# Retention, gated FFN and experts on one core: VectorE's and GpSimd's share of the side work, q's decay tables, and the pacing of the FFN

## The chip, the cores and the metric

One core of a Trainium2 chip runs the whole program. The metric is the device time of one execution in microseconds (us). Engines: PE is TensorE (PEld its weight loads), DVE is VectorE, ACT is ScalarE, POOL is GpSimd, SP is SyncE, whose queue issues almost every DMA. A matmul writes a PSUM bank of 128 x 512 floats; in this kernel VectorE and ScalarE read PSUM, and GpSimd works in SBUF alone.

## The reference

Three steps, each on the output of the one before:

```python
for t in range(S):                       # B=2, H=8, S=768, D=64
    state = gamma[None, :, None, None] * state + k_t v_t^T
    y[:, :, t] = scale * q_t @ state
x = y as (1536, 512)
xn = x / sqrt(mean(x * x) + 1e-6) * rms_g
x = (silu(xn @ w_gate) * (xn @ w_val)) @ w_out        # d_ff = 1536
p = probs / (probs.sum(-1) + 1e-9)                    # 4 experts, F = 1024
out = sum over e of p[:, e] * (relu(x @ w1[e]) @ w2[e])
```

## The kernel before, in words

The recurrence is computed in chunks of 128 tokens: 2 batches of 6 chunks, twelve in all (`NS`), i = 0 to 11. In each step i the program issues the scores of chunk i+1 (q times k, L631), masks them by VectorE (`am`, L639), and then mixes chunk i: masked scores times v (L660) plus q times the state S (L652), and the state's update (L688, copied to S by ScalarE, L696). Decay by position is kept in tables: `gk` scales k (L609), and `gq`, one 128 x 512 table for each of the last five chunks of a batch, scales q in place (`prep_q`, L620, by VectorE or GpSimd). The five `gq` tables come by five DMAs on SP's queue (L793, L826).

The norm of a chunk (`normal`, `normal2`) is a chain between ScalarE and VectorE: square and sum L674, root L676 and L678, VectorE's reciprocal L703, ScalarE's L706 to L708, and VectorE's product `xn` L714. `to_x` then transposes xn on PE (L736) into one of six PSUM banks, which are used in turn. The matmuls of the FFN are made from operands split in two: a high part (cast to fp32r) and a low part (value minus high part), so each product of two matrices is three matmuls. The tokens of a batch form two blocks of 384. A product over two blocks and two halves of the weights is done with seven smaller products instead of eight (the Winograd form, L449), which needs sums of pieces: `first` holds block 0 as copied out of PSUM (L745), `tsum` holds differences (L758, L760, L766, L770), and xX, xB22 and xT are the split operands (high L722 and L756, low L725 and L762; L725 is `split`).

Each weight tile arrives as 64-bit numbers in `wst` and is turned into high and low parts by a sequence: bits L301 (ScalarE); L304, L309, L315 and L322 `top` (VectorE); sums L338 and low parts `widelo`/`plainlo` L371 (VectorE or GpSimd); casts L366 (ScalarE). ScalarE's L458 copies a product's bank to `kept`; VectorE's L539, L509 and L542 add and multiply the products, L513 is the Silu, and L547 the low part of h. The output products are L966 to L968.

The order of such side work is written by a planner in the program, `Pace` (L32 to L137). It keeps a clock for each engine, moved on by `did` and `work` with costs from `COST`, and a clock `now` for PE, moved on by `matmuls`. Tasks wait in lists with the engines that may do them ("PV" is GpSimd or VectorE). `fill(span)` issues tasks that are ready and end within the span; `need` issues a task that must be done now, on the engine whose clock and cost are least. `ready` counts back a latency where a task follows one of its own engine. A task that uses the port that VectorE and GpSimd share (`port`) also starts no earlier than the other engine's last such task. Nothing is chosen at run time: the planner sets the order in which instructions stand on each engine.

The last two norms and the first products of the FFN overlap: from chunk 10 on, the first FFN unit's gate products fill PE between the mixes. The FFN has six units (`N1`) for each of two batches, twelve steps; the experts follow.

Of the kernel before, what the change touches and what calls it, by code (L numbers as in the profile page):

```python
# [31 lines left out]
class Pace:  # L32
# [6 lines left out]
    COST = {"A": (0.09, 0.00085), "V": (0.07, 0.00105), "P": (0.14, 0.00213), "D": (0.0, 0.0018)}  # L39
# [4 lines left out]
    def __init__(self, engines):  # L44
        self.engines = engines

        self.order = "DVAP"
        self.now = 0.0
        self.clock = dict.fromkeys("AVPD", 0.0)

        self.port = {"V": 0.0, "P": 0.0}
        self.waiting = [[], [], []]

    def cost(self, engine, size):
        fixed, each = self.COST[engine]
# [31 lines left out]
    def need(self, *tasks):  # L87

        for task in tasks:
            if task.end is None:  # L90
                self.need(*task.deps)
                engine = min(task.engines, key=lambda e: self.clock[e] + self.cost(e, task.size))
# [3 lines left out]
    def ready(self, task, engine):  # L96

        ends = [d.end - (self.LATENCY[engine] if d.engine == engine else 0.0) for d in task.deps]
# [4 lines left out]
    def can(self, task, engine):  # L103
        return (
# [49 lines left out]
def tile_retention_gated_experts(  # L154
# [16 lines left out]
    c_q: bass.AP,  # L171
    out: bass.AP,
# [11 lines left out]
    H = c_k.shape[2]  # L184
    S = NCH * CHUNK
# [379 lines left out]
    with ExitStack() as actx:  # L565
# [11 lines left out]

        rows = [wstage.tile([P, H, CHUNK], F32, tag="wst", name=f"rows{x}")[0:1] for x in range(2)]
        g_sb = ac.tile([P, DM], F32, name="g_sb")
# [8 lines left out]
        first_block = {}  # L588
# [25 lines left out]
        def prep_q(i):  # L614

            c = chunks[i][1]
            if c:
# [3 lines left out]
                    [pace.done(pace.now)],  # L621
                )

        def scores(i):
# [8 lines left out]
            st[i]["scores"], st[i]["am"] = ps, am  # L633
            prep_q(i)
# [95 lines left out]
        def to_x(i):  # L730
# [8 lines left out]
            if blk == 0:  # L739
# [4 lines left out]
                hi, lo = (x[:, :, cols] for x in xs[b]["X"])  # L744
                nc.scalar.copy(out=b1, in_=ps)  # L745
                done = pace.done(pace.did("A", DM))
                split(b, first_block[b, "readers"], [done], hi, lo, b1, DM)
# [37 lines left out]
        nc.scalar.dma_start(out=square, in_=c_square)  # L785
        nc.vector.memset(S_sb[0], 0.0)
# [6 lines left out]
        nc.sync.dma_start(out=gq[:, 0], in_=c_q[:, 0])  # L793
# [24 lines left out]
        for i in range(NS):  # L818
# [6 lines left out]
            if i < NCH - 2:  # L825
                nc.sync.dma_start(out=gq[:, i + 1], in_=c_q[:, i + 1])  # L826
# [50 lines left out]
        to_x(NS - 1)  # L877
        value = winograd(weights(("v", 0)), xs[0], value_use(silu[0], first_hs))
# [184 lines left out]
    for i, (u, g) in enumerate(steps):  # L1063
        hs = {} if i else first_hs
        if i:
# [53 lines left out]
def _constants(H, S, D):  # L1119

    import numpy as np
# [42 lines left out]
```

## Time and profile before

| what | value |
|---|---|
| three runs, median (lowest to highest) | 874.62 us (874.04 to 877.77) |
| the profiled execution | 874.55 us |
| its span, first to last instruction | 872.8 us |
| busy: PE / DVE / ACT / POOL | 852.2 / 574.1 / 375.5 / 302.5 us |
| mean granted TensorE clock | 0.994 |
| moved by DMA | 53.96 MB |

The span is what the trace covers; the execution's own time is 1.75 us longer. An idle bracket on a row tells how long that engine stood still before it and what ended the wait. [...] PE's rows overlap, so the distance between starts counts, not their length.

### The profile page before, as it was taken

What the parts mean: (1) busy time and instruction counts of PE and PEld (TensorE: products, weight loads), DVE (VectorE), ACT (ScalarE), POOL (GpSimd) and SP (SyncE); (2) the same over time, 40 slices, a digit from 0 to 9 for tenths busy, and PEclk for the clock granted to TensorE, in tenths of its full rate; (3) what the DMA queues carried; (4) which work ended last, traced back from release to release, by engine and by line L of the source; (5) the groups of instructions that cost most, each with busy time, mean ns of one, the idle gap of its engine ahead of it and who ended that gap; (6) DMA issues with size and microseconds to landing.
All of it is one profiled execution on the core that took longest, in us unless ns stands there. A gap on an engine that the chain in (4) does not pass through costs nothing.

```text
span 872.8 us, 12589 instructions
## 1 busy us (share of the span) xinstructions
PE 852.2 (98%) x4726; PEld 792.6 (91%) x4726; DVE 574.1 (66%) x1031; ACT 375.5 (43%) x838; POOL 302.5 (35%) x377
## 2 busy tenths in 40 slices
PE   9997999899999999999999999999999999999998
PEld 8887999899999999988998889998898889998897
DVE  4788967979796965943565665656556556555554
ACT  3786675445453536664333333233333333323221
POOL 2656774336373738661121122112012012211000
PEclk9999999999999999999999999999999999999999
DMA  8861232213130301010010011011001101101003
GB/s 285 270 213 39 73 97 73 73 50 97 30 116 25 97 25 37 13 48 25 25 49 26 24 49 37 15 47 49 25 25 49 31 18 49 37 13 49 24 5 141
DMA packets 33409, 53.96 MB, mean 62 GB/s; under 512 B 4418, under 2 KB 13506, under 8 KB 33348
## 3 DMA queue, kind: packets, MB, share of 16 engines
q1 hardware_dynamic: 33200, 53.01, 19.3%
q8 instruction: 37, 0.61, 0.3%
q14 instruction: 24, 0.20, 0.1%
q10 hardware_dynamic: 148, 0.14, 0.1%
HBM read 50.00 MB, written 3.15 MB: 61 GB/s over the span
## 4 chain that ended last, share of the span: by engine, by line
PE 85%; DVE 8%; ACT 3%; POOL 1%; issue 1%; DMA 1%; SPq 0%; DVEq 0%; ACTq 0%
PE bank L449 40%; PE bank L1035 10%; PE bank L1036 10%; PE bank L1034 10%; PE bank L967 3%; PE bank L968 3%; PE bank L966 3%; DVE s L542 2%; PE bank L660 1%; DMA q<-in_qt_dram 1%; POOL x2Tlo L919 1%; DVE kept L539 1%; PE bank L631 1%; PE bank L652 1%; DVE sums L338 1%
## 5 line engine op out<-in xcount | busy, mean ns | idle before, releaser
L1042 DVE SCALAR_TENSOR_TENSOR oacc<-bank,p_sb,oacc 128x512 f32<-128x512 f32 (+1 forms) x181 | 134.8, 745 | 67.2 <-PE bank L1036 67.2
L1035 PE MATMUL bank<-plainlo,hs 128*128 128x512 f32 (+1 forms) x386 | 151.5, 392 | 0.0
L1036 PE MATMUL bank<-plainhi,hs 128*128 128x512 f32 (+1 forms) x386 | 151.5, 392 | 0.0
L1034 PE MATMUL bank<-plainhi,hs 128*128 128x512 f32 (+1 forms) x386 | 150.8, 391 | 0.0
L458 ACT COPY kept<-bank 128x384 f32<-128x384 f32 x168 | 80.6, 480 | 155.3 <-PE bank L449 153.5
L999 DVE TENSOR_TENSOR kept<-bank,kept 128x384 f32<-128x384 f32 x96 | 53.5, 557 | 119.7 <-PE bank L449 89.3
L371 POOL TENSOR_TENSOR plainlo<-wst,plainhi 128x512 fp32r<-128x512 f32 x16 | 27.8, 1740 | 284.3 <-ACT plainhi L366 284.3
L371 POOL TENSOR_TENSOR widelo<-sums,widehi 128x512 fp32r<-128x512 f32 x40 | 51.9, 1298 | 114.9 <-ACT widehi L366 110.0
L1036 PEld LDWEIGHTS bank<-plainhi,hs 128*128 128x128 f32 x386 | 72.5, 188 | 16.1
L449 PE MATMUL bank<-x2Thi,widehi 128*128 128x384 f32 x256 | 86.3, 337 | 0.7 <-DVE kept L999 0.7
L449 PE MATMUL bank<-x2Thi,widelo 128*128 128x384 f32 x256 | 85.7, 335 | 0.0
L449 PE MATMUL bank<-x2Tlo,widehi 128*128 128x384 f32 x256 | 85.7, 335 | 0.0
L1035 PEld LDWEIGHTS bank<-plainlo,hs 128*128 128x128 f32 x386 | 72.4, 188 | 14.3 <-POOL plainlo L371 0.3
L1034 PEld LDWEIGHTS bank<-plainhi,hs 128*128 128x128 f32 x386 | 72.4, 188 | 14.0
L1002 ACT ACTIVATE hs<-kept 128x384 fp32r<-128x384 f32 x96 | 50.4, 525 | 77.0 <-DVE kept L999 76.9
L449 PE MATMUL bank<-xThi,widehi 128*128 128x384 f32 x192 | 65.4, 340 | 2.7 <-DVE s L509 1.0
L967 PE MATMUL bank<-hlo,plainhi 128*128 128x384 f32 x192 | 64.3, 335 | 1.1 <-POOL hlo L547 1.0
L449 PE MATMUL bank<-xThi,widelo 128*128 128x384 f32 x192 | 64.8, 337 | 0.0
L449 PE MATMUL bank<-xTlo,widehi 128*128 128x384 f32 x192 | 64.7, 337 | 0.0
L968 PE MATMUL bank<-hhi,plainlo 128*128 128x384 f32 x192 | 64.2, 335 | 0.0
L966 PE MATMUL bank<-hhi,plainhi 128*128 128x384 f32 x192 | 64.2, 334 | 0.0
L1006 DVE SCALAR_TENSOR_TENSOR hs<-kept,hs 128x384 fp32r<-128x384 f32 x96 | 53.0, 563 | 4.1 <-ACT hs L1002 4.1
(150 smaller groups left out, 1923.9 us busy)
## 6 DMA issues: line engine op xcount, KB each, us to landing
wst<-in_moe_w_dram SPq DMA_DIRECT2D x64, 256.0 KB, 2.7
wst<-in_moe_w_gate_dram SPq DMA_DIRECT2D x12, 512.0 KB, 3.7
wst<-in_moe_w_val_dram SPq DMA_DIRECT2D x12, 512.0 KB, 3.8
wst<-in_moe_w_out_dram SPq DMA_DIRECT2D x12, 512.0 KB, 3.3
v<-in_vn_dram SPq DMA_DIRECT2D x12, 256.0 KB, 5.0
kn<-in_kn_dram SPq DMA_DIRECT2D x12, 256.0 KB, 3.7
q<-in_qt_dram SPq DMA_DIRECT2D x11, 256.0 KB, 4.4
k<-in_kt_dram SPq DMA_DIRECT2D x11, 256.0 KB, 4.6
```

What stands on the lines that cost most here:

```text
L371: eng.tensor_tensor(out=at(lo), in0=t, in1=at(hi).bitcast(F32), op=ALU.subtract)
L449: nc.tensor.matmul(out=ps, lhsT=lhs, rhs=rhs, start=(first and j == i == 0), stop=(j == KH - 1 and i == 2), skip_group_check=not first,)
L458: nc.scalar.copy(out=t, in_=ps)
L966: nc.tensor.matmul(out=ps, lhsT=whi[:, c], rhs=hi, start=(f == 0), stop=False)
L967: nc.tensor.matmul(out=ps, lhsT=whi[:, c], rhs=lo, start=False, stop=False)
L968: nc.tensor.matmul(out=ps, lhsT=wlo[:, c], rhs=hi, start=False, stop=(f == NF - 1))
L999: nc.vector.tensor_tensor(out=t, in0=a, in1=t, op=ALU.add)
L1006: lambda eng: eng.scalar_tensor_tensor(out=lo, in0=t, scalar=0.0, in1=hi.bitcast(F32), op0=ALU.max, op1=ALU.subtract), [high],
L1034: nc.tensor.matmul(out=ps, lhsT=hi[:, c], rhs=whi[:, cols], start=(f == 0), stop=False)
L1035: nc.tensor.matmul(out=ps, lhsT=hi[:, c], rhs=wlo[:, cols], start=False, stop=False)
L1036: nc.tensor.matmul(out=ps, lhsT=lo[:, c], rhs=whi[:, cols], start=False, stop=(f == NF - 1))
L1042: nc.vector.scalar_tensor_tensor(out=acc, in0=ps, scalar=pe, in1=acc, op0=ALU.mult, op1=ALU.add)
```

## The change

Five edits. (1) In block 0 the low part is taken on VectorE alone, straight from the bank of the transposes, and so is the cast of the high part on ScalarE; the copy `first` stays. (2) The five `gq` tables are no longer loaded: two small inputs are (20 rows of decays, split in a high and a low part, and a matrix that picks rows), cast by ScalarE, and for i = 0 to 4 one matmul with 20 rows of contraction writes a 128 x 512 table in a bank, which ScalarE copies to `gq`. `prep_q` comes after it. (3) `pace.hold`, from the mix of chunk 10 to the last `to_x`: VectorE takes no task on the shared port that GpSimd could do. (4) `pace.tight` off in all FFN units but the last: DMAs cost 0.0029 per column in place of 0.0018, `need` looks at the clocks alone, and no latency is counted back. (5) With `tight` on, `need` also counts when a task is ready.

```diff
-    COST = {"A": (0.09, 0.00085), "V": (0.07, 0.00105), "P": (0.14, 0.00213), "D": (0.0, 0.0018)}
+    COST = {"A": (0.09, 0.00085), "V": (0.07, 0.00105), "P": (0.14, 0.00213), "D": (0.0, 0.0018), "late D": (0.0, 0.0029)}
@@ cost
-        fixed, each = self.COST[engine]
+        fixed, each = self.COST[engine if self.tight else engine.replace("D", "late D")]
@@ need
-                engine = min(task.engines, key=lambda e: self.clock[e] + self.cost(e, task.size))
+                engine = min(
+                    task.engines,
+                    key=lambda e: max(self.clock[e], self.ready(task, e) if self.tight else 0.0) + self.cost(e, task.size),
+                )
@@ ready
-        ends = [d.end - (self.LATENCY[engine] if d.engine == engine else 0.0) for d in task.deps]
+        ends = [d.end - (self.LATENCY[engine] if self.tight and d.engine == engine else 0.0) for d in task.deps]
@@ can
+        if engine == "V" and self.hold and task.port and "P" in task.engines:
+            return False
@@ to_x, block 0
+                where = banks.readers[-1]
+                high = pace.add(1, "A", DM, lambda eng: eng.copy(out=hi, in_=ps), [pace.done(pace.now)])
+                low = pace.add(
+                    1, "V", DM, lambda eng: eng.tensor_tensor(out=lo, in0=ps, in1=hi.bitcast(F32), op=ALU.subtract),
+                    [high], port=False,
+                )
                 nc.scalar.copy(out=b1, in_=ps)
-                done = pace.done(pace.did("A", DM))
-                split(b, first_block[b, "readers"], [done], hi, lo, b1, DM)
+                pace.did("A", DM)
+                where += [high, low]
+                x_tasks[b] += [high, low]
                 return
@@ start
+        nc.scalar.dma_start(out=flat[:, 0:NP], in_=c_q)
+        nc.scalar.dma_start(out=flat[:, NP:NP + NCH - 1], in_=c_pick)
...
-        nc.sync.dma_start(out=gq[:, 0], in_=c_q[:, 0])
@@ chunk i
-            if i < NCH - 2:
-                nc.sync.dma_start(out=gq[:, i + 1], in_=c_q[:, i + 1])
...
+                nc.scalar.copy(out=q_rows, in_=flat[:, 0:NP])
+                nc.scalar.copy(out=picks, in_=flat[:, NP:NP + NCH - 1])
...
                 scores(i + 1)
+                if i < NCH - 1:
+                    ps = pairs(bank())
+                    nc.tensor.matmul(out=ps, lhsT=picks[:, i], rhs=q_rows, start=True, stop=True)
+                    pace.matmuls(0.23)
+                    nc.scalar.copy(out=gq[:, i], in_=ps)
+                    gq_end[i] = pace.did("A", DM)
+                prep_q(i + 1)
                 masked(i + 1)
...
+            pace.hold = i >= NS - 2
             mix(i)
...
         to_x(NS - 1)
+        pace.hold = pace.tight = False
@@ FFN steps
+        pace.tight = u == N1 - 1
```

The changed file's lines are numbered 11 to 34 higher, so that L703 becomes L716, L509 L520, L539 L550. VectorE at the last norm, before, from the first difference of the FFN's first unit (L509) to the reciprocal and the weight steps behind it:

```order
L509 TENSOR_TENSOR s<-bank,kept 128x384
L766 TENSOR_TENSOR tsum<-tsum,first 128x256
L770 TENSOR_TENSOR tsum<-first,tsum 128x256
L371 TENSOR_TENSOR widelo_811<-top,widehi_810 128x2x128
L371 TENSOR_TENSOR widelo_811<-top,widehi_810 128x128
L371 TENSOR_TENSOR widelo_811<-sums,widehi_810 128x4x128
L703 RECIPROCAL r_1026<-r_1025 128x1
L304 SCALAR_TENSOR_TENSOR wst<-bits,wst 128x512
L309 TENSOR_SCALAR bits<-wst 128x512
```

The same place in the changed kernel (L520 is the difference, L716 the reciprocal):

```order
L520 TENSOR_TENSOR s<-bank,kept 128x384
L333 SCALAR_TENSOR_TENSOR top<-wst,bits 128x512
L716 RECIPROCAL r_1051<-r_1050 128x1
L779 TENSOR_TENSOR tsum<-bank,first 128x256
L781 TENSOR_TENSOR tsum<-bank,tsum 128x256
L783 TENSOR_TENSOR xB22lo_91<-bank,xB22hi_90 128x2x128
L727 SCALAR_TENSOR_TENSOR xn<-bank,r_1051,g_sb 128x512
```

Two tsum steps and three widelo are gone from ahead of the reciprocal; one weight step (`top`) has come there. GpSimd from the sums before the last norms on, before:

```order
L725 TENSOR_TENSOR xTlo_87<-tsum,xThi_86 128x4x128
L338 TENSOR_TENSOR sums<-top,sums 128x128
L725 TENSOR_TENSOR xXlo_89<-first,xXhi_88 128x4x128 x3
L725 TENSOR_TENSOR xTlo_93<-tsum,xThi_92 128x4x128 x2
L766 TENSOR_TENSOR tsum<-tsum,first 128x256
L770 TENSOR_TENSOR tsum<-first,tsum 128x256
L766 TENSOR_TENSOR tsum<-tsum,first 128x256
L725 TENSOR_TENSOR xTlo_93<-tsum,xThi_92 128x4x128
```

and in the changed kernel:

```order
L382 TENSOR_TENSOR widelo_666<-top,widehi_665 128x2x128
L382 TENSOR_TENSOR widelo_666<-top,widehi_665 128x128
L382 TENSOR_TENSOR widelo_666<-sums,widehi_665 128x4x128
L738 TENSOR_TENSOR xTlo_87<-tsum,xThi_86 128x4x128 x2
L787 TENSOR_TENSOR tsum<-tsum,first 128x256
L791 TENSOR_TENSOR tsum<-first,tsum 128x256
L738 TENSOR_TENSOR xTlo_93<-tsum,xThi_92 128x4x128
L787 TENSOR_TENSOR tsum<-tsum,first 128x256
L791 TENSOR_TENSOR tsum<-first,tsum 128x256
```

Its low parts of block 0 (xXlo) are gone, and three widelo of the weight and both tsum steps of each chunk stand there. VectorE in the FFN, from the L539 that starts at 137.83 in the trace of before:

```order
L539 TENSOR_TENSOR kept<-bank,kept 128x384
L542 TENSOR_TENSOR s<-kept,s 128x384
L322 SCALAR_TENSOR_TENSOR top<-wst,bits 128x512
L338 TENSOR_TENSOR sums<-top 128x128
L338 TENSOR_TENSOR sums<-sums,top 128x128
L338 TENSOR_TENSOR sums<-top 128x128
L338 TENSOR_TENSOR sums<-top,sums 128x128
L547 TENSOR_TENSOR hlo<-s,hhi 128x384
L539 TENSOR_TENSOR kept<-bank,kept 128x384
L542 TENSOR_TENSOR s<-kept,s 128x384
```

and in the changed kernel (L550 is that line):

```order
L550 TENSOR_TENSOR kept<-bank,kept 128x384
L553 TENSOR_TENSOR s<-kept,s 128x384
L333 SCALAR_TENSOR_TENSOR top<-wst,bits 128x512
L550 TENSOR_TENSOR kept<-bank,kept 128x384
L553 TENSOR_TENSOR s<-kept,s 128x384
L550 TENSOR_TENSOR kept<-bank,kept 128x384
L553 TENSOR_TENSOR s<-kept,s 128x384
L349 TENSOR_TENSOR sums<-sums,top 128x128
```

Between the first two `kept` only `top` is left; the sums stand elsewhere, and so does the low part L547, which GpSimd now does.

## Rows read from the trace of the kernel before

**Rows 1.** The page, busy time of each engine (us, share of the span, instructions).

```profile
PE 852.2 (98%) x4726; PEld 792.6 (91%) x4726; DVE 574.1 (66%) x1031; ACT 375.5 (43%) x838; POOL 302.5 (35%) x377
```

**Rows 2.** PE's waits: what was waited for, us in total, times, longest.

```profile
PE bank L449 <- ACT kept L458: 6.7, 4, 4.8
PE bank L631 <- DMA q<-in_qt_dram: 1.9, 3, 1.1
```

**Rows 3.** PE over time: start, us, engine, line, operation, form, [idle before <-releaser].

```profile
83.61 0.69 PE L449 MATMUL bank<-xB22hi,widehi 128*128 128x384 f32 x1 [4.83 <-ACT kept L458]
...
144.87 0.44 PE L449 MATMUL bank<-xThi,widehi 128*128 128x384 f32 x1 [0.77 <-DVE kept L539]
...
153.64 0.44 PE L449 MATMUL bank<-xThi,widehi 128*128 128x384 f32 x1 [1.00 <-DVE s L509]
...
165.96 0.45 PE L449 MATMUL bank<-xB22hi,widehi 128*128 128x384 f32 x1 [0.56 <-ACT kept L458]
...
168.28 0.49 PE L449 MATMUL bank<-xThi,widehi 128*128 128x384 f32 x1 [0.98 <-ACT kept L458]
```

**Rows 4.** The chain that ended last, in order of time: start, us, what.

```profile
77.77 4.37 DVE widelo L371 x3
...
83.61 3.74 PE bank L449 x12
...
135.63 2.10 PE bank L449 x12
...
168.28 10.16 PE bank L449 x48
```

**Rows 5.** VectorE over time, 73 to 84 us.

```profile
76.26 1.51 DVE L770 TENSOR_TENSOR tsum<-first,tsum 128x256 f32<-128x256 f32 x1
...
82.06 0.15 DVE L703 RECIPROCAL r<-r 128x1 f32<-128x1 f32 x1
```

**Rows 6.** The tile `first`: its instructions, duration ns min/median/max, first and last start.

```profile
L745 ACT COPY first<-bank x6: 586/586/587, 21.5 to 66.3; 128x512 f32<-128x512 f32 x6
...
L770 DVE TENSOR_TENSOR tsum<-first,tsum x2: 410/958/1506, 54.2 to 76.3; 128x256 f32<-128x256 f32 x2
L725 DVE TENSOR_TENSOR xXlo<-first,xXhi x1: 686/686/686, 37.3 to 37.3; 128x512 fp32r<-128x512 f32 x1
```

**Rows 7.** GpSimd over time, 73 to 84 us.

```profile
74.78 4.14 POOL L725 TENSOR_TENSOR xXlo<-first,xXhi 128x512 fp32r<-128x512 f32 x3
```

**Rows 8.** ScalarE over time, 77 to 87 us.

```profile
77.80 0.62 ACT L722 CAST xThi<-tsum 128x512 fp32r<-128x512 f32 x1 [1.98 <-DVE tsum L770]
78.33 0.59 ACT L674 ACTIVATE xn<-bank 128x512 f32<-128x512 f32 x1
...
82.24 0.20 ACT L706 ACTIVATE r<-r 128x1 f32<-128x1 f32 x1 [2.72 <-DVE r L703]
```

**Rows 9.** VectorE over time, 135 to 143 us.

```profile
137.83 0.56 DVE L539 TENSOR_TENSOR kept<-bank,kept 128x384 f32<-128x384 f32 x1 [4.67 <-PE bank L449]
...
139.64 0.67 DVE L322 SCALAR_TENSOR_TENSOR top<-wst,bits 128x512 uint32<-128x512 uint32 x1
...
142.57 0.54 DVE L539 TENSOR_TENSOR kept<-bank,kept 128x384 f32<-128x384 f32 x1
```

**Rows 10.** Stretches: length, PE, PEld, DVE, ACT, POOL busy us, PEclk, DMA share, GB/s.

```profile
20.00:35.00 15.00, 13.71 (x137) 12.71 (x137) 9.60 (x21) 12.25 (x37) 7.32 (x8) 1.00 0.95 295
35.00:50.00 15.00, 13.53 (x134) 12.38 (x133) 13.33 (x25) 9.90 (x31) 12.20 (x14) 1.00 0.60 208
140.00:165.00 25.00, 23.23 (x130) 22.15 (x130) 24.55 (x49) 11.67 (x28) 10.81 (x12) 1.00 0.25 78
200.00:326.00 126.00, 125.77 (x724) 125.03 (x723) 100.37 (x183) 57.09 (x124) 64.81 (x85) 1.00 0.21 64
```

**Rows 11.** DMA issues, KB each, median us to landing.

```profile
gq<-in_c_q_dram SPq DMA_DIRECT2D x5, 256.0 KB, 5.3
```

**Rows 12.** The tile `am`: its instructions, duration ns min/median/max.

```profile
L639 DVE TENSOR_TENSOR am<-bank,mask x24: 669/682/692, 9.6 to 67.9; 128x512 f32<-128x512 f32 x24
```

More of the change, by code (lines that the diff above doesn't have):

```diff
@@ L47, in __init__ @@
         self.order = "DVAP"
+        self.hold = False
+        self.tight = True
         self.now = 0.0
@@ L171, in tile_retention_gated_experts @@
     c_q: bass.AP,
+    c_pick: bass.AP,
     out: bass.AP,
@@ L184, in tile_retention_gated_experts @@
     H = c_k.shape[2]
+    NR = c_q.shape[0]
     S = NCH * CHUNK
@@ L578, in tile_retention_gated_experts @@
         rows = [wstage.tile([P, H, CHUNK], F32, tag="wst", name=f"rows{x}")[0:1] for x in range(2)]
+        q_rows = ap2.tile([P, 2 * KD, P], F32R, tag="tsum", name="q_rows")[0:NR, 0:NP]
+        picks = ap2.tile([P, 2 * KD, P], F32R, tag="tsum", name="picks")[0:NR, 0:NCH - 1]
         g_sb = ac.tile([P, DM], F32, name="g_sb")
@@ L587, in tile_retention_gated_experts @@
         st = [dict() for _ in range(NS)]
-        first_block = {}
+        first_block, gq_end = {}, {}
         def pairs(ps):
@@ L620, in prep_q @@
                     0, "PV", DM, lambda eng: eng.tensor_tensor(out=t, in0=t, in1=gq[:, c - 1], op=ALU.mult),
-                    [pace.done(pace.now)],
+                    [pace.done(max(st[i]["q free"], gq_end[c - 1]))],
                 )
@@ L632, in scores @@
             pace.matmuls(1.15, st[i]["q end"], st[i]["k end"])
-            st[i]["scores"], st[i]["am"] = ps, am
-            prep_q(i)
+            st[i]["scores"], st[i]["am"], st[i]["q free"] = ps, am, pace.now
         def masked(i):
@@ L785, in tile_retention_gated_experts @@
         nc.scalar.dma_start(out=square, in_=c_square)
+        loaded = ap2.tile([P, KD, TB], F32, tag="first", name="rows_q", bufs=1)[0:NR]
+        flat = loaded.rearrange("p n t -> p (n t)").rearrange("p (n c) -> p n c", c=CHUNK)
+        nc.scalar.dma_start(out=flat[:, 0:NP], in_=c_q)
+        nc.scalar.dma_start(out=flat[:, NP:NP + NCH - 1], in_=c_pick)
         nc.vector.memset(S_sb[0], 0.0)
@@ L1131, in _constants @@
     by_k = (gamma ** -pos[:, None]).reshape(NCH, CHUNK, H).transpose(1, 0, 2)
-    by_q = (gamma ** pos[:, None] / np.sqrt(D)).reshape(NCH, CHUNK, NP, 2)[1:].transpose(3, 0, 2, 1)
-    by_q = np.repeat(by_q, D, axis=0)
-    return [np.ascontiguousarray(x).astype(np.float32) for x in (rows, square, by_k, by_q)]
+    by_q = (gamma ** pos[:, None] / np.sqrt(D)).reshape(NCH, CHUNK, NP, 2)[1:].transpose(0, 3, 2, 1)
+    by_q = by_q.reshape(2 * (NCH - 1), NP, CHUNK).astype(np.float32)
+    hi = (by_q.view(np.uint32) & np.uint32(0xFFFFF000)).view(np.float32)
+    by_q = np.concatenate([hi, by_q - hi])
+    pick = np.zeros((NCH - 1, 2, NCH - 1, 2, D))
+    for c in range(NCH - 1):
+        for j in range(2):
+            pick[c, j, c, j] = 1.0
+    pick = np.concatenate([pick.reshape(2 * (NCH - 1), NCH - 1, 2 * D)] * 2)
+    return [np.ascontiguousarray(x).astype(np.float32) for x in (rows, square, by_k, by_q, pick)]
 def kernel(**inputs):
@@ L1151 @@
         laid[n + "n"] = inputs[n].reshape(B, H, NCH, CHUNK, D).transpose(0, 2, 3, 1, 4).reshape(B, NCH, CHUNK, DM)
-    consts = zip(("c_rows", "c_square", "c_k", "c_q"), _constants(H, S, D))
+    consts = zip(("c_rows", "c_square", "c_k", "c_q", "c_pick"), _constants(H, S, D))
     nc = _bacc.Bacc("TRN2", target_bir_lowering=False, num_devices=1)
```

## The prediction

> **What bounds the kernel now.** The profiled execution took 874.55 us, of which 872.8 are the span; the other 1.75 us lie around it. The median of the three runs, 874.62 us, is 0.07 us away, so the sum below is made against 874.55 and stands for the median too. I began with busy times: TensorE (PE) is busy for 852.2 of 872.8 us [rows 1], so no edit to another engine shortens anything unless it removes one of PE's 20.6 us of idle time, or time that PE spends at a lower clock. So the second view was PE's waits by releaser: 6.7 us for ScalarE's copies `kept`, 1.9 for loads of q [rows 2]. The third was PE's own rows that carry an idle bracket [rows 3]: one stall of 4.83 us ends at 83.61; four smaller ones, 0.77, 1.00, 0.56 and 0.98, end at 144.87, 153.64, 165.96 and 168.28, 3.31 us together. Fourth, the chain that ended last [rows 4]: twelve FFN products took 2.10 us at 135.63 but 3.74 at 83.61, right behind the long stall: PE had stood still, its granted clock is below full there, and that costs 1.64 us. Likewise 48 products at 168.28 took 10.16 us where 48/12 x 2.10 = 8.40 are due: 1.76 us more, behind two stalls 2.3 us apart. Behind the lone stalls of 0.77 and 1.00 no such loss shows.
>
> The cause of the long stall is in the rows of the other engines. VectorE runs `tsum` L770 for 1.51 us from 76.26, then three conversions of weights that the chain puts at 4.37 us [rows 4], and only at 82.06 the reciprocal L703 [rows 5]. The same L770 takes 0.41 us at its shortest [rows 6], and GpSimd was at work on xXlo from 74.78 for 4.14 us [rows 7]: two SBUF inputs on VectorE beside SBUF work on GpSimd, and VectorE's take up to 3.7 times as long. ScalarE pays twice: `xThi` waits 1.98 us for that tsum, so the norm's square starts at 78.33 only, and its L706 waits 2.72 us for the reciprocal [rows 8]. The copy `kept`, for which PE waits, stands behind L708 on ScalarE.
>
> **The change, part by part.** (1) The hold, with the low parts of block 0. In the new order VectorE has one step of a weight conversion (the `top` of 0.67 us [rows 9]) between the difference L509 and the reciprocal; tsum and the three widelo go to GpSimd, which loses its three xXlo. So `xThi` need not wait: the square starts 1.98 us sooner, at 76.35 [rows 8]. From the square to PE's return it was 83.61 - 78.33 = 5.28 us; without the 2.72 it is 2.56, so PE returns at 78.91. The stall began at 83.61 - 4.83 = 78.78 [rows 3], so 0.1 us of it would stay; I take 0.3, for the casts that ScalarE now has in other places. So 4.5 go, and with so short a stop the 1.6 us of lower clock too. Term: **-6.1**. Bounds: if tsum on GpSimd comes no sooner than it did on VectorE, only the 2.72 go (-2.7); at best all of 4.83 + 1.64 (-6.5). I take a value near the best, since in the new order the widelo of that weight stand on GpSimd ahead of the last two tsum steps, in the place of the three xXlo.
>
> (2) The older pacing in the FFN, 100 to 175 us. VectorE is busy for 24.55 of the 25 us of 140 to 165 [rows 10], but before 137.83 it had sat idle for 4.67 us [rows 9]. The weight steps could run there and did not, for the planner starts a step only when its own clocks say so. In the new order the steps stand earlier: between the first two `kept` shown VectorE had `top`, four sums and hlo, from 139.64 to 142.57, 2.93 us [rows 9], and now has `top` alone (0.67): 2.26 us sooner, more than the stall of 0.77 behind it. The lead carries on to 153.64, whose 1.00 goes as well, and to 165.96 (0.56). The 0.98 at 168.28 I leave: there ScalarE follows an s on VectorE that runs beside GpSimd's SBUF work, which stays on GpSimd. So 0.77 + 1.00 + 0.56 = 2.33, and with the pair of stalls broken the 1.76 of clock: **-4.1**. Bounds: 0 (a new order can fall as badly) to -(3.31 + 1.76) = -5.1.
>
> (3) q's tables. Removed: five loads of 256 KB that took 5.3 us each to land [rows 11], in a stretch where the DMA engines are 95% busy [rows 10]; SP's queue then issues the loads of q behind them sooner, and two small loads go out on ScalarE's queue. PE waited 1.9 us for q [rows 2]; I take -1.2, bounds 0 and -1.9. Added: five products of 512 columns on PE, 0.175 x 512/384 = 0.23 us each, +1.15, all on the path since PE is full; five ScalarE copies of 0.59 us [rows 6], 2.9 us in 0 to 40 us, where ScalarE has 12.25 of 15 us busy in 20 to 35 [rows 10]. They lie beside PE's work as long as the weight casts, which the planner may move, make room; if not, each delays S or the norm, and PE by up to 0.59: +2.9. GpSimd's or VectorE's scaling of q now waits for the copy; its user S x q comes behind the next product group, and PE meets the copy first there.
>
> (4) Low part of block 0 on VectorE. Six subtractions from PSUM of 0.68 us (the masked scores `am` have that form, 682 ns [rows 12]) replace one on VectorE (686 ns [rows 6]) and five on GpSimd: 3.4 us more for VectorE in 20 to 70 us, where it is busy for 9.60 of 15 us at first, but for 13.33 of 15 from 35 to 50 [rows 10], part of it moved away by the planner. Behind each on its engine stand `am` and the next norm; `am` is asked for a chunk later, so it hides. What is new: a PSUM bank of transposes is free only when VectorE has read it, not when ScalarE has, and with the table's bank five instead of four of the six banks turn per chunk. Bounds: 0 to one subtraction per chunk, 6 x 0.69 = +4.1; I take +0.05, since a bank comes up again only five or six fills later, most of a chunk. Parts (3) and (4): -1.2 + 1.15 + 0.05 = **0.0**. Bounds: at best all of q's 1.9 goes and the products lie in waits that PE has there anyway (-1.9); at worst no load comes sooner and half of 4.1 and 2.9 stops PE, the products lying inside those stops (+3.5).
>
> [...]
>
> (5) From 175 to 326 us the steps stand in another order too, but PE is busy for 125.77 of the 126 us from 200 on [rows 10]: nothing to gain, 0.0; what it may lose is rival D. From about 326 us on, the order is the same on every engine, so the rest of the 20.6 us stays.
>
> Sum: 874.55 - 6.1 - 4.1 + 0.0 = 864.35, **864.4 us**.
>
> **The rivals.** A (0.10): the banks. If VectorE's low part comes late enough to hold the transposes' bank each time, six chunks stop PE by a subtraction (0.69) and what stands ahead of it, 1 us in all: 864.4 + 6 = 870.4. For it: VectorE's 13.33 of 15 us from 35 on [rows 10]. Against: it had 5.4 of 15 us free just before.
> B (0.08): the older pacing merely moves the FFN's stalls: 864.4 + 4.1 = 868.5. For it: the number of weight steps is the same. Against: 4.67 us of idle VectorE [rows 9] are there to be filled.
> C (0.08): the hold makes GpSimd the late engine. tsum then ends on GpSimd when it ended on VectorE, only the 2.72 us go, and the clock falls as before: 864.4 + 3.4 = 867.8. [...]
> D (0.05), the other side: in 175 to 326 us VectorE now carries steps that the trace of before has earlier or later, in a period of 46.2 us (one FFN unit, two batches). If the older pacing puts three late differences in each of the three periods, as 140 to 170 us has them now, each period costs 3.31 + 1.76 = 5.1 us, 15.2 in all: 864.4 + 15.2 = 879.6. It decides once VectorE is late by more than the lead of a `kept` in every period. Against: PE lost 0.23 us in 126 there [rows 10].
>
> **How the numbers follow.** The forecast has 0.69. About 0.5% (4.4 us) can be told from no change here: under 870.2 is faster, over 879 slower. Forecast, B and C are faster, but a little of the forecast's spread (attention at +3.5 with another term at its poor end) passes 870.2: 0.69 + 0.16 - 0.03 = 0.82. A and that 0.03 are the same: 0.13. D: 0.05. The range: the best ends, -6.5 - 5.1 - 1.9 = -13.5, give 861.0, and I go 1.5 further down for PE's other stops before 70 us, which I did not cost; at the far end it takes in A, 870.4, and 1.1 for a part that does worse beside it: 859.5 to 871.5. Left out are D, the worst of the forecast's spread and what I have overlooked.
>
> **What would show it.** Right: no idle bracket of over 1 us at PE near 75 to 80 us; ScalarE's L706 counterpart not waiting for the reciprocal; twelve products there at 0.175 us each; 140 to 175 us at granted clock 1.00; q's waits under 1 us in all; five table products at 0.23 us. Wrong: PE rows from 15 to 70 us that wait for the low part on VectorE (A), for ScalarE's copies of the tables, or stalls of over 0.5 us between 175 and 326 (D).

## The result and the profile after

The changed kernel took 867.76 us (median of 4, 864.96 to 868.06) beside 876.19 for the kernel before (4 runs): a ratio of 0.989 with an interval of 0.9844 to 0.9937. Measured again with more runs it was 864.93 (6 runs, 864.3 to 867.88) beside 875.39 (11 runs), 0.9894 (0.9871 to 0.9917). The predicted 864.4 is 0.5 us under the second and 3.4 under the first; why the two differ is told with the start of the program below. The profiled execution took 867.49 us, with this span and these busy times (page, as rows 1):

```profile
span 865.7 us, 12619 instructions
...
PE 853.1 (99%) x4731; PEld 793.1 (92%) x4731; DVE 574.6 (66%) x1054; ACT 378.3 (44%) x845; POOL 280.8 (32%) x354
```

PE's idle time fell from 20.6 to 12.6 us. PE's rows with an idle bracket of 0.4 us or more between 45 and 330 us, which answer to [rows 3]:

```profile
47.10 0.63 PE L749 MATMUL bank<-square,xn 128*128 128x128 f32 x4 [0.87 <-DVE xn L727]
...
53.95 0.46 PE L665 MATMUL bank<-S,q 128*128 128x128 f32 x2 [0.73 <-ACT S L709]
...
90.46 0.44 PE L460 MATMUL bank<-xB22hi,widehi 128*128 128x384 f32 x1 [0.47 <-ACT kept L469]
...
191.90 0.44 PE L460 MATMUL bank<-xB22hi,widehi 128*128 128x384 f32 x1 [0.81 <-ACT kept L469]
...
239.24 0.44 PE L460 MATMUL bank<-xB22hi,widehi 128*128 128x384 f32 x1 [0.82 <-ACT kept L469]
```

The stop of 4.83 us is gone and so are the four of 140 to 170; in their place stand shorter ones, two of them, 0.81 and 0.82, where the kernel before had none. Stretches of the changed kernel (columns as in [rows 10]):

```profile
80.00:90.00 10.00, 9.92 (x58) 8.97 (x56) 6.49 (x13) 8.27 (x21) 5.49 (x6) 1.00 0.18 54
140.00:165.00 25.00, 24.89 (x144) 24.57 (x143) 23.18 (x43) 13.39 (x30) 17.18 (x25) 1.00 0.24 79
165.00:175.00 10.00, 10.00 (x60) 10.00 (x59) 8.13 (x16) 5.61 (x11) 3.40 (x3) 1.00 0.36 106
200.00:326.00 126.00, 125.14 (x718) 124.22 (x718) 102.49 (x199) 58.20 (x129) 55.55 (x69) 1.00 0.21 66
```

PE's granted clock (PEclk, a share of full speed) is 1.00 in all of them, and VectorE has 23.18 of 25 us busy in 140 to 165 in place of 24.55.

To compare kernels whose early part differs, I cut PE's time at four marks: its first transposes of a chunk, its last ones, the seventh group of FFN output products and the nineteenth.

| kernel | first transposes at | stretch 1 | stretch 2 | stretch 3 | 2 + 3 | stop near the last norm |
|---|---|---|---|---|---|---|
| before | 20.39 | 66.79 | 91.09 | 138.69 | 229.78 | 4.83 |
| changed | 24.04 | 60.09 | 85.96 | 140.16 | 226.12 | none |

Difference by stretch: +3.65 before the first transposes, -6.70, -5.13, +1.47, and -0.39 behind 310 us: -7.1 in all, the difference of the two spans. One more measure looks at the last norm alone: from PE's transposes before the last to the last ones it is 10.06 us in the kernel before and 4.06 in the changed one, with the same products between. Waits for q lie ahead of it, so it compares kernels that differ there.

### The profile page after: what moved, and what is told of

Its sections match the earlier page's. It is cut to its first block, busy times and chain, and to the rows that moved or that the text cites. A ratio compares the mean times of both kernels' runs of the same rounds, so it can differ in the third digit from the quotient of the medians.

```text
span 865.7 us, 12619 instructions
## 1 busy us (share of the span) xinstructions
PE 853.1 (99%) x4731; PEld 793.1 (92%) x4731; DVE 574.6 (66%) x1054; ACT 378.3 (44%) x845; POOL 280.8 (32%) x354
## 4 chain that ended last, share of the span: by engine, by line
PE 88%; DVE 5%; ACT 3%; POOL 2%; issue 1%; DMA 0%; DVEq 0%; ACTq 0%; SPq 0%; POOLq 0%
PE bank L460 41%; PE bank L1069 10%; PE bank L1070 10%; PE bank L1068 10%; PE bank L1001 3%; PE bank L1002 3%; PE bank L1000 3%; PE bank L673 1%; DVE s L553 1%; PE bank L665 1%; POOL x2Tlo L953 1%; PE bank L645 1%; DVE kept L550 1%; PE state L701 1%; DMA kn<-in_kn_dram 0%
## 5 line engine op out<-in xcount | busy, mean ns | idle before, releaser
L382 POOL TENSOR_TENSOR widelo<-sums,widehi 128x512 fp32r<-128x512 f32 x37 | 48.4, 1308 | 112.7 <-ACT widehi L377 112.3
L558 POOL TENSOR_TENSOR hlo<-s,hhi 128x384 fp32r<-128x384 f32 x44 | 47.0, 1071 | 33.5 <-ACT hhi L555 26.8
```

The costliest lines, as they stand in the source:

```text
L382: eng.tensor_tensor(out=at(lo), in0=t, in1=at(hi).bitcast(F32), op=ALU.subtract)
```

## The experiments

Three kernels put one part alone into the kernel before, four take one part out of the changed kernel, two look at the start, and three at combinations.

**The hold alone, on the kernel before** (`pace.hold` and its lines in `can`, with the reset behind the last `to_x`, and nothing else).

> The kernel before with the hold alone (VectorE takes no shared task from the mix of chunk 10 to the last transposes). Measure: stretch 1, from PE's first transposes of a chunk to those of the last (66.79 us before, 60.09 in the changed kernel); stretch 2, from there to the seventh group of output products of the FFN (91.09 and 85.96); stretch 3, from there to the nineteenth group (138.69 and 140.16). My theory: the long stall is weight work on VectorE ahead of the reciprocal, which the hold alone moves to GpSimd. The stall of 4.83 falls under 2, stretch 1 is 3 to 5 us shorter, stretches 2 and 3 within 0.7 of before. Rival (the hold needs GpSimd to be rid of the low parts of block 0): tsum comes late on GpSimd instead, stretch 1 within 1 us of before.

Measured: 873.96 us (9 runs, 869.35 to 875.88) beside 876.45; no stop near the last norm, which took 4.05 us in place of 10.06; stretches 64.51, 91.28, 138.69. VectorE there (L512 is L509, L706 the reciprocal L703):

```profile
81.41 0.68 DVE L307 SCALAR_TENSOR_TENSOR wst<-bits,wst 128x512 f32<-128x512 f32 x1
82.12 0.69 DVE L312 TENSOR_SCALAR bits<-wst 128x512 uint32<-128x512 uint32 x1
82.85 0.69 DVE L318 SCALAR_TENSOR_TENSOR bits<-wst,bits 128x512 uint32<-128x512 uint32 x1
83.46 0.16 DVE L706 RECIPROCAL r<-r 128x1 f32<-128x1 f32 x1
```

Three weight steps stand there, 0.7 us each, and the reciprocal follows them at once. So my theory held on the stop and its rival fell. Stretch 1 is only 2.3 us shorter, less than the 3 to 5 that I expected, because this execution waited 2.43 us for q at 36.56 and PE's clock was lower behind it (0.89 in the mean):

```profile
40.00:60.00 20.00, 18.36 (x158) 17.13 (x158) 15.10 (x31) 11.87 (x37) 12.96 (x16) 0.89 0.57 185
```

This execution also had the late start that is told with the start of the program below (first scores at 8.87 us; 6.94 in the profile of before). The median is only 2.5 us under that of before, so other executions too seem to have lost part of the 6.0; where, no run shows.

The FFN's stops are all there, as expected, here the last pair. But the products behind that pair ran at the full clock (1.00 from 170 to 175 us): 36 of them in 6.51 us by the chain, 0.18 each.

```profile
167.60 0.44 PE L452 MATMUL bank<-xB22hi,widehi 128*128 128x384 f32 x1 [0.58 <-ACT kept L461]
...
169.91 0.44 PE L452 MATMUL bank<-xThi,widehi 128*128 128x384 f32 x1 [0.99 <-ACT kept L461]
```

```profile
169.91 6.51 PE bank L452 x36
```

**The low parts alone, on the kernel before** (the `to_x` part of the diff above and nothing else).

> The kernel before with the low parts of block 0 on VectorE from PSUM, and nothing else. My theory: GpSimd, rid of three subtractions, gets the weights' low parts by the planner's own costs, so that the reciprocal is early without a hold: stretch 1 is 4 to 6 us shorter than the 66.79 of before. Rival 1 (the hold does it): stretch 1 within 1 us of before. Rival 2 (the bank of the transposes is held until VectorE has read it): PE waits for the low part in 15 to 70 us, 0.7 us or more in each of several chunks, and stretch 1 is longer by 2 us or more.

Measured: 867.55 us (6 runs, 865.47 to 872.03) beside 876.45, ratio 0.9908 (0.9874 to 0.9942): most of the whole change's gain from one part. No stop near the last norm, which took 4.05 us; stretches 66.13, 87.40 and 138.66. My theory was right on the stop, and rival 2 (the bank) fell, since no wait of PE names the low part. Stretch 1 by itself came out as rival 1 wanted, 0.7 us shorter and not 4 to 6; but rival 1 meant that the stop stays, and it went. What stretch 1 gained there it lost to q, twice: PE's waits for q, and the stretch of 40 to 60 us with the clock at 0.74.

```profile
PE bank L631 <- DMA q<-in_qt_dram: 3.4, 3, 1.7
```

```profile
40.00:60.00 20.00, 17.86 (x131) 16.58 (x128) 13.46 (x27) 10.78 (x32) 12.05 (x14) 0.74 0.53 182
```

Not foreseen was that stretch 2 fell by 3.7 us, with the pacing of the kernel before.

**The older pacing alone, on the kernel before** (`late D`, no latency counted back, in all FFN units but the last).

> The kernel before with the older pacing in the FFN alone (all units but the last). My theory: it puts the weight steps where VectorE sat idle, so stretch 2 (91.09 before) is 4 to 5.5 us shorter, stretch 3 (138.69) longer by 0 to 1.6, stretch 1 the same. Rival (the FFN's gain came from the attention part, which left more of the weights converted): stretch 2 within 1 us of before.

Measured: 873.14 us (9 runs, 869.1 to 876.18) beside 876.45; stretch 2 is 85.79 and stretch 3 137.71, together 6.3 us shorter than before. My theory held on stretch 2 and its rival fell. Stretch 3, which I had at 0 to 1.6 us longer, is 1.0 shorter, and stretch 1, expected the same, is 71.95 in place of 66.79, for this execution waited 3.4 us for q and lost PE's clock between 40 and 60 us (0.74):

```profile
40.00:60.00 20.00, 17.71 (x131) 16.35 (x130) 15.36 (x30) 11.57 (x36) 12.63 (x15) 0.74 0.55 184
```

Attention's order is that of before, so it is also a control: the long stop stands there to the hundredth, and the twelve products behind it take 4.22 us by the chain, slow again [rows 4]; the last norm took 10.48 us.

```profile
90.69 0.69 PE L450 MATMUL bank<-xB22hi,widehi 128*128 128x384 f32 x1 [4.83 <-ACT kept L459]
```

**The changed kernel without the hold** (the line `pace.hold = i >= NS - 2` removed).

> The changed kernel without the hold. VectorE then has two tsum steps, a low part and one weight step between the first difference of the FFN and the last reciprocal. My theory (VectorE's list ahead of the reciprocal sets the stall): those with two SBUF inputs stretch beside GpSimd, and PE stands still for 1 to 3 us near 79, stretch 1 is 1.5 to 4 us longer than the 60.09 of the changed kernel. Rival (the low parts in PSUM do all of it): stretch 1 within 0.5 us of the changed kernel.

Measured: 867.24 us (3 runs, 865.76 to 867.27); a stop of 1.00 us at 81.96, stretch 1 60.84, stretches 2 and 3 together 226.17. The stop is at the lower end of my range, stretch 1 below it: the two tsum steps on VectorE took 0.41 and 0.42, and GpSimd stood idle beside them. The hold is worth 0.75 us here.

**The changed kernel with q's tables loaded as before** (the five DMAs back; the small loads, casts and products out).

> The changed kernel with q's tables loaded by five DMAs on SP's queue as before, without the five table products and their copies. My theory: PE's waits for loads of q come back, 1.5 to 3.5 us in all before 75 us, and in some executions the granted clock falls between 40 and 60 us (0.74 to 0.9 over that stretch), which adds 3 to 5 us there; the products, 0.41 us from start to start each in the changed kernel, are saved (2.05). So an execution that keeps its clock is within 1.5 us of the changed kernel, one that loses it 2 to 5 us slower, and the median is slower by 1 to 3. Rival (the products cost more than the loads): no wait for q over 0.5 us, 1 to 2 us faster.

Measured: 866.45 us (9 runs, 863.41 to 871.82). PE waits for q again, and loses its clock in 40 to 60 us, where the changed kernel keeps it:

```profile
PE bank L641 <- DMA q<-in_qt_dram: 2.3, 2, 2.1
```

```profile
40.00:60.00 20.00, 18.36 (x147) 17.10 (x147) 13.00 (x28) 11.26 (x34) 10.00 (x14) 0.82 0.56 185
```

The changed kernel:

```profile
40.00:60.00 20.00, 18.22 (x182) 16.87 (x182) 17.09 (x37) 15.15 (x46) 11.41 (x16) 1.00 0.69 232
```

The waits came as my theory said. A slower median was not shown: the ratio to before is 0.9881 (0.985 to 0.9912) beside the changed kernel's 0.9894. The best execution, 863.41, is better than any of the changed kernel's ten (864.3 at best), the worst, 871.82, is 3.8 us worse than theirs. What the tables on PE are seen to buy is a narrower spread.

**The changed kernel with the newer pacing in all of the FFN.**

```diff
-        pace.hold = pace.tight = False
+        pace.hold = False
...
-        pace.tight = u == N1 - 1
```

This is not quite the FFN of the kernel before, since `need` here counts when a task is ready (the fifth edit).

> The changed kernel with the newer pacing in all of the FFN. Stretches as before: 1 from PE's first to its last transposes (60.09 us in the changed kernel), 2 from there to the seventh group of output products (85.96), 3 from there to the nineteenth (140.16). Theory A (the older pacing made the gain in the FFN): stretch 2 goes back to 89 us or more, stretch 3 to 138.7; 2.5 us slower or more. Theory B (the low parts alone already move the weight steps, as the kernel before with the low parts alone showed with 87.40 and 138.66): stretches 2 and 3 together within 1 us of the changed kernel's 226.12. Stretch 1 within 0.5 us in both.

Measured: 865.48 us (3 runs, 865.26 to 868.23); stretches 59.93, 87.78, 138.66: 226.44 for 2 and 3, 0.3 from the changed kernel. Theory B. With the low parts in, the older pacing takes 1.8 us from stretch 2 and adds 1.5 to stretch 3. The low parts alone, with the FFN's pacing exactly as before, had 226.06.

**The changed kernel with block 0's low parts as before** (`split` from the copy in SBUF; tables, hold and older pacing kept).

> The changed kernel with block 0's low parts as before (from the copy in SBUF, on GpSimd or VectorE), with the tables, the hold and the older pacing. Theory A (the hold and the low parts do the same thing, either is enough): no stall over 1.2 us between 75 and 90 us, stretch 1 within 1.5 us of the changed kernel's 60.09; stretches 2 and 3 between the 223.5 of the kernel before with the older pacing alone and the 226.1 of the changed kernel. Theory B (GpSimd, with the three subtractions back, makes tsum late): a stall of 1.5 us or more there, with a lower clock behind it.

Measured: 865.19 us (3 runs, 862.19 to 865.52); no stop near the last norm; stretches 59.42, 84.63, 140.20. Theory A. With the same late start as the changed kernel (first scores at 8.87 us in both) its span is 863.4 beside 865.7: the low parts on VectorE cost 2.3 us where the rest is in, 0.4 of it ahead of the first transposes, 0.7 in stretch 1 and 1.3 in stretch 2. The other two times are in line with that: 865.52 and 862.19, where the changed kernel's two groups of times (below) lie at 867.49 to 868.06 and 864.3 to 865.13. One place can be read off. In the changed kernel the low part stands ahead of `am` and of the norm's product, for which PE waits 0.87 us at 47.10; without it PE waits 0.61.

```profile
44.43 0.67 DVE L762 TENSOR_TENSOR xXlo<-bank,xXhi 128x512 fp32r<-128x512 f32 x1
45.02 1.28 DVE L652 TENSOR_TENSOR am<-bank,mask 128x512 f32<-128x512 f32 x2
46.21 0.74 DVE L727 SCALAR_TENSOR_TENSOR xn<-bank,r,g_sb 128x512 f32<-128x512 f32 x1
```

**Sixteen idle products at the start** (`WARM` 16, the later eight removed).

> The changed kernel with the eight idle products that stand behind the first mix's preparation moved to the start, so that sixteen run there in a row. In the profile of the changed kernel PE's first products ran at the lower clock until about 10.9 us, in that of before until 5 to 7 us. Theory A (the level follows what PE did from its first product on): it rises at the same time whatever the product, the first scores of chunk 0 run at the upper level, the first transposes stand at 21 to 24 us. Theory B (it rises at a time that differs from execution to execution): the first transposes stand anywhere between 21 and 25 us and the times spread by 3 us as in the changed kernel. Theory C (loads of the next chunk are late once nothing fills the time): a wait of PE for q or k of 1 us or more ahead of the second scores.

Measured: 865.55 us (3 runs, 864.45 to 868.67), first transposes at 25.28 us. PE's first rows:

```profile
8.11 2.05 PE L832 MATMUL bank<-rows,rows 1*128 1x128 f32 x16
10.09 3.02 PE L645 MATMUL bank<-q,k 64*128 64x128 f32 x32
...
13.76 3.68 PE L673 MATMUL bank<-v,am 128*128 128x64 f32 x16
```

```profile
11.00:13.00 2.00, 2.00 (x22) 1.81 (x18) 1.55 (x3) 0.59 (x1) 0.06 (x1) 0.50 0.48 162
```

The 32 scores are those of chunks 0 and 1. The first sixteen run at the upper level, as theory A wanted (granted clock 0.99 from 9 to 11 us). Then the level falls, with PE never idle: the clock is 0.50 from 11 to 20 us, and the mix takes 3.68 us for 16 products beside 2.00 in the changed kernel. So theory A fell in its second half, and C fell, since PE waits for nothing there. Theory B is not shown either: the transposes stand 0.3 us outside its band, and they are late here because the level fell again, not because it rose late.

**The changed kernel again.**

> The changed kernel once more, unaltered, for its spread on this chip. The theory on the start (PE's clock rises early or late by chance of the execution, whichever kernel it is): times in two groups about 2.7 us apart, near 865.0 and 867.8, and a profile whose first scores stand at either 7 or 8.9 us; the stretches from the first transposes on as in the first profile (60.09, 85.96, 140.16) within 0.5 us. Rival (the change itself brings the late rise): first scores at 8.9 in all.

Measured: five runs from 864.3 to 865.13 and one of 867.88; with the first four runs of this kernel, six within 864.3 to 865.13 and four within 867.49 to 868.06, nothing between. This profile's first scores stand at 7.25 us in place of 8.87; its stretches (59.90, 85.97, 140.24) are those of the first. PE at the start in this execution:

```profile
5.17 2.16 PE L832 MATMUL bank<-rows,rows 1*128 1x128 f32 x16
7.25 1.16 PE L645 MATMUL bank<-q,k 64*128 64x128 f32 x16
```

and in the first profile of the same kernel:

```profile
5.16 3.78 PE L832 MATMUL bank<-rows,rows 1*128 1x128 f32 x16
8.87 2.08 PE L645 MATMUL bank<-q,k 64*128 64x128 f32 x16
```

The same sixteen products took 2.16 us in one and 3.78 in the other. The theory held, the rival fell; among the kernels without the change's tables, too, first scores stand at 6.94 us in the kernel before and at 8.87 with the hold alone. But the level does not simply rise once. In this execution it fell again behind the scores, for the sixteen idle products of L862 (11.63 - 8.35 = 3.3 us), with PE never idle:

```profile
9.00:11.00 2.00, 2.00 (x11) 2.00 (x11) 1.97 (x4) 0.82 (x2) 1.04 (x1) 0.50 0.94 328
```

In the kernel before, too, the clock is 0.50 from 9 to 11 us, then 0.87 from 11 to 13 and 1.00 from 13 to 16. In the first profile of the changed kernel the same idle products take 3.58 us from start to start, up to 14.46; the sixteen of the kernel before take 3.61 from 8.03 on, where the clock reads 0.50. So I take the lower level to last to 14.46 without a break there, though the windows of that profile read 1.00.

**Tables and older pacing alone** (the changed kernel with the old low parts and no hold; the change to `need` is in).

> The changed kernel with block 0's low parts as before and without the hold: tables and older pacing alone. Two tsum steps and two low parts, all with two SBUF inputs, stand on VectorE between the first difference of the FFN and the last reciprocal. Theory A (hold and low parts are each enough, and one of them is needed): a stall of 2.5 to 5 us near 80, with a lower clock behind it if it is the longer; stretch 1 is 2.5 to 6.5 us longer than the 59.4 of the kernel with the hold and old low parts. Rival (the planner puts the work well enough once the tables are gone from the queues): no stall over 1 us, same time within 1.

Measured: 863.47 us (6 runs, 860.51 to 865.4) beside 875.39, 0.987 (0.9846 to 0.9894); a stop of 0.96 us, stretch 1 60.21, stretches 2 and 3 together 223.41. Theory A fell in its second half: with neither hold nor new low parts the long stop still does not come back, as the rival said. The older pacing begins only behind the last `to_x`, and alone it had kept the stop, so the tables or the change to `need` took it; no run parts these two. VectorE, and GpSimd beside it:

```profile
77.39 0.42 DVE L779 TENSOR_TENSOR tsum<-tsum,first 128x256 f32<-128x256 f32 x1
77.73 1.79 DVE L738 TENSOR_TENSOR xXlo<-first,xXhi 128x512 fp32r<-128x512 f32 x1
79.44 0.41 DVE L783 TENSOR_TENSOR tsum<-first,tsum 128x256 f32<-128x256 f32 x1
79.78 0.68 DVE L738 TENSOR_TENSOR xXlo<-first,xXhi 128x512 fp32r<-128x512 f32 x1
80.38 0.15 DVE L716 RECIPROCAL r<-r 128x1 f32<-128x1 f32 x1
```

```profile
73.49 1.78 POOL L738 TENSOR_TENSOR xXlo<-first,xXhi 128x512 fp32r<-128x512 f32 x1
77.41 1.56 POOL L738 TENSOR_TENSOR xTlo<-tsum,xThi 128x512 fp32r<-128x512 f32 x1 [2.15 <-ACT xThi L735]
```

Four steps with two SBUF inputs do stand ahead of the reciprocal, but only the one that overlaps GpSimd's 1.56 us stretched (1.79 in place of 0.67 to 0.69); the tsum steps ran in 0.42 and 0.41. GpSimd had done the weight's three low parts by 73.5. By these rows, what stopped PE in the kernel before was not this kind of step as such but five of them in a row, the weight's three among them, beside GpSimd's 4.14 us of [rows 7] and the two low parts that it took behind them.

**The older pacing in the first two units, old low parts**

```diff
-        pace.tight = u == N1 - 1
+        pace.tight = u >= 2
```

> The changed kernel with the old low parts, and the older pacing in the FFN's first two units alone (newer from the third). The kernel before has no stall over 0.25 us between 178 and 326 with the newer pacing, and the older one has two of 0.82 there. My theory: stretch 3 is 138.7 (140.20 with the older pacing), stretch 2 stays at 84.6, so 1.5 us faster than with the older pacing throughout: 863.7 or 861.0, late or early clock at the start. Rival (the planner's state at the switch carries other stalls along): stretch 3 within 0.4 of 140.2 or longer.

Measured: 863.62 us (5 runs, 861.7 to 864.2) beside 875.39, 0.987 (0.9848 to 0.9892); span 862.4 with the late start; stretches 59.31, 84.61, 138.73, no stop over 0.4 us between 25 and 330. My theory, to 0.1 us in the stretches; the profiled time, with the late start, is 864.2 beside the 863.7 expected. It and the kernel before this one are the best of the study, 1.3 and 1.5 us under the changed kernel's median in the same series. The intervals of the ratios overlap; the firmer evidence is stretches 2 and 3, 223.34 and 223.41 beside 226.12. All five times of this kernel lie under the changed kernel's lowest, 864.3.

**And in the first unit alone** (`u >= 1`).

> The same with the older pacing in the first unit alone (newer from the second). The pair to the run with two units: theory A (what the older pacing gives, it gives by steps moved forward in the first unit, in VectorE's idle time before 138 us): stretches 2 and 3 as there, 223.3 together, within 0.5. Theory B (it is needed through the second unit too, where VectorE was saturated): stretch 2 is 1 us or more longer than 84.6, up to the 87.8 of the newer pacing throughout.

Measured: 866.52 us (6 runs, 865.63 to 869.55), stretch 2 89.22, stretch 3 138.70. Theory B, by more than its upper end of 87.8: the four stops of before are back (0.76, 0.96, 0.57, 0.98), though not the loss of clock behind them (1.00 from 135 to 175 us).

## Why the prediction was right, and where its steps were not

The time, 864.4, was met within 0.6 us by the second measurement and within 3.4 by the first; the direction and the range held. That the sum came out so close is in part luck: stretch 2 gave 1.0 us more than its term, stretch 3 took 1.5 that had stood at nothing, and the rest of the program gave 0.4. By its steps:

- **Part (1), -6.1.** From the transposes before last (77.12 and 80.07) to the last (87.18 and 84.13) PE needs 10.06 us before and 4.06 after: -6.0. The chain of steps was the forecast one: one weight step stands ahead of the reciprocal, ScalarE's L719 no longer waits for it, and the reciprocal waits for ScalarE instead. From the square (79.17) to PE's next FFN product (81.78) it is 2.61 us, where the prediction had 2.56.

```profile
78.10 0.55 DVE L520 TENSOR_TENSOR s<-bank,kept 128x384 f32<-128x384 f32 x1
78.57 0.68 DVE L333 SCALAR_TENSOR_TENSOR top<-wst,bits 128x512 uint32<-128x512 uint32 x1
80.22 0.17 DVE L716 RECIPROCAL r<-r 128x1 f32<-128x1 f32 x1 [0.97 <-ACT r L689]
```

```profile
77.89 0.62 ACT L735 CAST xThi<-tsum 128x512 fp32r<-128x512 f32 x1 [0.83 <-DVE tsum L781]
79.17 0.60 ACT L687 ACTIVATE xn<-bank 128x512 f32<-128x512 f32 x1 [0.66 <-PE bank L673]
...
80.42 0.20 ACT L719 ACTIVATE r<-r 128x1 f32<-128x1 f32 x1
...
81.27 0.46 ACT L469 COPY kept<-bank 128x384 f32<-128x384 f32 x1
```

  xThi waits 0.83 in place of 1.98, and the square starts when PE has ended the mix, not when tsum comes [rows 8]. The size was right; the credit was not. I gave it to the hold with the low parts. The runs show that the hold alone, the low parts alone, or neither of them (tables, older pacing and `need`) each take the stop to 1.0 us or none, and only the run that left attention's order as it was kept it. It was one unlucky placement by the planner, which every change of the tasks around it that was tried removed; beside the other parts the hold itself is worth 0.75 to 0.8 us.
- **Part (2), -4.1.** Stretch 2 gave -5.1, the best end of the bounds: the 0.98 that I left went too. VectorE's idle time ahead of the counterpart of the L539 at 137.83 fell from 4.67 to 1.04 us, as the argument wanted, and alone the older pacing gave 6.3 over stretches 2 and 3.

```profile
135.49 0.56 DVE L550 TENSOR_TENSOR kept<-bank,kept 128x384 f32<-128x384 f32 x1 [1.04 <-PE bank L460]
```

  But the low parts alone gave 3.7, and beside them the pacing gives 0.3. Here too the terms do not add: with the new low parts, stretches 2 and 3 together are 226.06 to 226.44 in all six kernels, whatever the pacing; with the old ones they are 223.34 to 224.83 in the four whose older pacing reaches the second unit, and 227.92 or more in the other three. The term was met, but in the changed kernel the low parts had already taken it.
- **Part (5), 0.0.** This step was wrong: stretch 3 is 1.47 longer, and two stops of over 0.5 us between 175 and 326, which the prediction named as a sign against it, are there. The mechanism is rival D's at a tenth of its size. GpSimd does a sum behind a low part of h, ScalarE's cast waits for it, and `kept` stands behind the cast (GpSimd's rows, then ScalarE's):

```profile
189.37 1.02 POOL L558 TENSOR_TENSOR hlo<-s,hhi 128x384 fp32r<-128x384 f32 x1 [1.09 <-issue]
190.35 0.46 POOL L349 TENSOR_TENSOR sums<-top,sums 128x128 f32<-128x128 f32 x1
```

```profile
190.85 0.62 ACT L377 CAST widehi<-sums 128x512 fp32r<-128x512 f32 x1 [0.53 <-POOL sums L349]
191.37 0.47 ACT L469 COPY kept<-bank 128x384 f32<-128x384 f32 x1
```

  PE waits 0.81 at 191.90 for that copy. With the old low parts, the newer pacing from the third unit on removes it.
- **Part (3).** The waits for q went entirely (-1.9, I took -1.2). A product cost more than I made it: from its start to the next it is 0.41 or 0.42 us for the first three, not 0.23, and 0.55 and 0.86 for the last two (in the 0.86 PE waits 0.37 for ScalarE), so five cost 2.66 and not 1.15; the first two put the first transposes 0.83 later.

```profile
15.56 0.49 PE L868 MATMUL bank<-q_rows,picks 20*128 20x512 f32 x1
15.97 2.00 PE L673 MATMUL bank<-v,am 128*128 128x64 f32 x16
```

  I had scaled a stream of equal products; these lone ones between groups of other shapes are dearer. The two errors have opposite signs. The scores of chunk 1 start at 11.64 before and at 14.46, 2.82 later by the late start alone; the transposes before last stand at 77.12 and 80.07, 2.95 later: attention between cost +0.13, against 0.0 for parts (3) and (4).
- **Part (4), +0.05.** No wait of PE for a bank appeared, so rival A fell; but the low parts cost 2.3 us, which I had taken to hide. In attention VectorE's list shows it (the rows from 44.43 on); of the 1.3 in stretch 2 the stop of 0.47 at 90.46 is one piece, which the kernel with the old low parts does not have, and the rest is not traced. The six took 0.67 to 0.69 us each from PSUM; the one on VectorE from SBUF in the kernel before took 0.69 [rows 6].
- **Rivals B and C** fell by their times. B's mechanism is what the pacing does beside the low parts, where it moves time from stretch 2 to stretch 3; its condition, that the stops of 140 to 170 stay, was not met. For C speaks that VectorE's steps with two SBUF inputs can take longer beside GpSimd's: the step of 128x256 took 0.41 us alone and 1.51 beside GpSimd's work in the kernel before, the one of 128x512 0.68 and 1.79 in the kernel of tables and older pacing alone. The program calls what the two share a port; no run shows more of it than these times. But GpSimd's list was not late at the last norm: it stood idle for 1.57 us before its tsum at 77.94.

The reading by stretches makes +3.65 ahead of the first transposes the largest error: 2.82 of it is the pace of PE's products at the start, which differs between executions of one kernel (2.16 and 3.78 us for the same sixteen), and 0.83 the first two table products. My 874.55 came from an execution with the early start; the first profile of the changed kernel had the late one, and 867.49 - 2.8 = 864.7.

## What to carry to other kernels

A stop that comes from where a planner happened to put a few tasks can go away with many an edit (here with every one that moved those tasks), so its price must not be added up over the parts of a change: run each part alone, and keep one run that leaves the place as it was. Here the part that seemed the core (low parts out of PSUM) helped most alone and cost 2.3 us once the others were in, and the two best kernels of the study drop it. A part may also be worth its spread rather than its median, as the tables seem to be, by ten executions with them and nine without: what they remove are stops of which only some executions pay with their clock (0.74 to 0.89 between 40 and 60 us in four profiles, 1.00 in that of the kernel before).

## What had not been expected of the hardware

PE's pace at the start: the same sixteen products behind the first sixteen took 2.05 us in the kernel before, 2.16 in one execution of the changed kernel and 3.78 in the other, and the rest follows 2.5 to 2.8 us later; the kernel's times fall in two groups, 864.3 to 865.13 and 867.49 to 868.06. Only one execution of each group has a profile, so that the start parts the groups rests on these two. Where the pace rises early the clock falls again, to 0.50 between 9 and 11 us in the kernel before and in the second profile of the changed one, though PE has no idle time; with the later idle products moved to the start it stayed at 0.50 from 11 to 20 us. What decides either is open. The windows show a granted clock of 1.00 up to 7 us in either case, and throughout in the late execution, so there the spacing of products is the witness, not that column, and that it is the clock is my reading.

The clock behind a stop is not the same each time either. Behind the stop of 4.83 us it was 0.50 from 84 to 86 us in the kernel before. Behind the same pair of stops, 0.56 to 0.58 and 0.98 to 0.99 us, 48 products lost 1.76 us in the kernel before (clock 0.72 from 168 to 174 us); in the runs with the hold alone and with the older pacing in one unit the clock stayed at 1.00 up to 175 us, and the first 36 of them took 6.51 us in each. So the 1.76 in the prediction's part (2) is what that execution paid, not a price of the kernel; what decides it stays open. The same holds for the waits for q in attention: the kernel before's profile kept its clock between 40 and 60 us (1.00), four kernels with the same loads had 0.74 to 0.89 there.
